# Block-decay attention into an ELU feed-forward layer: the state term on 64x64 array tiles, states without zero blocks, and one sum read from PSUM

## The chip, the core and the metric

One core of a Trainium2 chip. TensorE (PE) multiplies, with the weight loads listed apart (PEld); VectorE (DVE) and ScalarE (ACT) read PE's results out of PSUM; GpSimd (POOL) works on SBUF and issues most loads; SyncE (SP) issues stores and DMA transposes. The metric is device time of one run in microseconds, lower is better.

## The reference

q, k, v are [4, 8, 768, 64] (batch, head, position, channel), lam [8], w_in [512, 2048], w_out [2048, 512], all float32. Per batch and head, over blocks of 64 positions:

```python
intra = (q_b k_b^T * Dmask) v_b             # Dmask[i, j] = lam**(i-j) for i >= j, else 0
inter = (q_b * lam**(pos+1)) @ kv_state
out_b = intra + inter
kv_state = lam**block * kv_state + (k_b * lam**(block-1-pos))^T v_b
```

The result, as x [3072, 512] (batch and position by head and channel), goes through `g = elu(x @ w_in)` and `g @ w_out`.

## The kernel before

**Chunks.** The kernel works in blocks of 128 positions: 6 blocks for each of 4 batches give 24 chunks g, with block g // 4 and batch g % 4. Chunks 0 to 3 stand alone; from 4 on two neighbours form a pair with a common tile xt. Heads lie in pairs (hp 0 to 3, hh 0 or 1): head 2*hp + hh sits in partitions hh*64 onward of column block hp.

**Steps of a chunk or pair**, by the token that stands for each in the program list:
- loads of q, k, v (cast to fp16 by the DMA), issued on POOL;
- `T`: q and k transposed by PE and evicted by DVE (qT, times the decay qs) and ACT (kT), for chunks up to 7; from chunk 8 on two DMA transposes on SP, issued with `W`;
- `W`: those transposes, kd = k times decay on POOL (L176), and the scaled old state stt (L390, on POOL in four ops of 64 partitions, from chunk 12 on ACT, L383);
- `S`: 16 score matmuls per pair (L304), masked by DVE into pp (L320);
- `B` or `P`, the burst: for each hp two matmuls of v by pp (L340) and, from chunk 4 on, two of the state by qT (L346), into one PSUM bank psO per chunk; then U, the state's increment (L417), one bank per pair. The evictions are xt (L361 on ACT, from chunk 8 L363 on DVE, times qs) and the new state st (L440, two ops of 64 partitions);
- `1:g:j`: x @ w_in (L660) into a bank psH of two, then exp (L666) and relu (L667) on ACT, and min(e - 1, relu) on DVE (L626), giving g or gg;
- the product with w_out: `2:g:j`, plain, 16 matmuls of 512 columns per chunk (L685), evicted by ACT (L700); or, for the pairs in SEVEN (8 to 22 before), `7:g:i`.

A state tile st is [128, hp, 128]: for a head pair the two 64x64 states stand on the diagonal and the other two blocks are zeros, written at the start (`z`, L202 and `Z`, L704). So one state matmul contracts over 128 partitions, half of them against zeros.

**Seven products.** For a pair the product with w_out is a 2x2 block product (two chunks by two halves of w_out's columns, over two halves of the inner blocks) done by seven block products in the order M3, M4, M5, M2, M1, M7, M6, of 8 matmuls with 256 columns each (L549). The left sides are gg and its sums P (for M5, M2), E (for M1) and D (for M7, M6), by DVE or by POOL as SHARED says for each pair (L500, L497). The right sides wf are sums of w_out (`F` on DVE, `G` on POOL, L517). M5 is added in PSUM onto M3, M2 onto M4 and M6 onto M1. On the way: ACT copies M3, M4 and M1 to SBUF (L556) and M3+M5, M4+M2 into the output tile osb (L566); POOL makes t = M3 + M4 and two differences s1, s2 (L562); DVE makes w1 = s1 + M1 (L562), and the last two corners w1 - M7 and s2 + (M1+M6) from PSUM (L579).

**What sets the order.** Every engine works in the order of the program list: FIRST and OPEN, written by hand, then `1:` in order with one product token behind each, and the other steps set in at fixed distances (AT, in numbers of `1:` steps) before the pair that needs them. POOL's early order is POOL_ORDER (q, k, v loads, i and o for parts of w_in and w_out, d for kd, m for stt). DVE work that may wait stands in three lists (`late`, `slow`, `later`) of which `flush` takes some at each product token. psO, psS, psU, psT and psM share banks A to D, M0, M1 by BANKS. SP's queue follows the program: a store there waits for its data and holds what stands behind it.

Of the kernel before, what the change touches and what calls it, by code (L numbers as in the profile page):

```python
# [15 lines left out]
def kernel(  # L16
# [15 lines left out]
    L = 128  # L32
# [11 lines left out]
    WI = [2] * 8  # L44
    WO = [2] * 8
    POOL_ORDER = (
        "q1 k0 iota k2 k1 q2 v0 v1 i0 i1 v2 i3 i2 o0 o1 d0 k3 q3 i4 i5 d1 o2 d2 o3 d3 o4 v3 o5 "
        "i6 i7 k4 o7 o6 q4 k6 m4 v4 q6 d5 d4 q8 q10 k8 d6 v6 v8 d7 v10 k10 m6"
# [4 lines left out]
        "z3 z0 z1 Z2 Z1 z2 Z0 T0 T1 S0 S1 T2 P0 P1 S2 1:0:0 U0 1:1:0 P2 1:1:1 1:2:0 2:0:0 "  # L53
        "1:2:1 2:1:0 1:0:1 T3 2:2:0 1:0:2 S3 1:2:2 2:2:1 U1 1:1:2 2:1:1 2:0:1 P3 2:0:2 1:3:0 "
        "2:1:2 1:1:3 M 1:2:3 Z3 2:2:2 1:3:2 U2 1:3:1 2:1:3 1:0:3 T4 T5 2:2:3 1:3:3 S4:5 2:3:0 "
        "2:0:3 2:3:2 U3 F0 B:P4:P5:U4:U5 M 2:3:3 1:4:1 T6 1:4:0 G3 T7 2:3:1 G4 W9 1:4:3 G5 G1 "
        "S6:7 1:4:2 G2 2:5:0 2:4:0 1:4:4 1:4:5 W8 B:P6:P7:U6:U7 L12 1:4:7 1:6:1 2:5:1 2:4:1 G7 "
        "1:4:6 1:6:0 G6 2:4:2 S8:9 1:6:2 1:6:4 2:5:2 2:5:3 W11 1:6:3 1:6:6 B:P8:P9:U8:U9 1:6:7 "
        "2:4:3 1:6:5 W10"
# [4 lines left out]
    DELAY = 0  # L64
    COMB = nc.gpsimd

    SEVEN = (8, 10, 12, 14, 16, 18, 20, 22)
    SHARED = {8: 'D', 10: 'ED', 12: 'ED', 14: 'ED', 16: '', 18: '', 20: '', 22: 'ED'}
    AT = {'L': -19, 'l': 1, 'W': -13, 'T': -5, 'S': -7, 'B': -5}
    BANKS = (  # L70
        "S0=M0,A S1=D,C S2=D,M1 S3=D,B P0=M1 P1=M0 P2=B P3=A U0=B U1=B U2=B U3=M1 T0=M1,D "
        "T1=D,C T2=M0,D T3=B T4=B T5=D T6=M1 T7=D M2=C M3=M0"
# [19 lines left out]

    stp = [
        [cpool.tile([128, 2, NHP, 128], FP16, name=f"st{x}_{i}") for i in range(2)]
# [5 lines left out]
    def emit_load(w, g0):  # L100
        n = size_of[g0]
        c, b = divmod(g0, B)
        x = {"q": q, "k": k, "v": v}[w]
        src = x[b : b + n, :, c * L : (c + 1) * L].rearrange("b h p d -> p (b h) d")
        t = asb.tile([128, n, H, 64], FP16, tag=f"{w}n{n}", name=f"{w}n{g0}", bufs=4)
        {"q": qg, "k": kg, "v": vg}[w][g0] = t
        nc.gpsimd.dma_start(out=t[:].rearrange("p b h d -> p (b h) d"), in_=src)  # L107
# [38 lines left out]
    def emit_wi(i):  # L146
        written.add(("i", i))
        f0 = sum(WI[:i]) * 128
        nc.gpsimd.dma_start(  # L149
            out=wi16[i][:],  # L150
            in_=moe_w_in[:, f0 : f0 + WI[i] * 128].rearrange("(k p) f -> p k f", p=128),
        )
# [48 lines left out]
    def zero_st1(b):  # L201
        nc.vector.memset(st[b][1], 0.0)  # L202

# [8 lines left out]

    dn = cpool.tile([128, H], FP32, name="dn")
    mask = cpool.tile([128, H, 128], FP32, name="mask")
    qs = cpool.tile([128, NHP, 128], FP32, name="qs")
    ks = cpool.tile([128, H], FP32, name="ks")
# [11 lines left out]
    for hh in range(2):  # L228
        r = slice(hh * 64, (hh + 1) * 64)
        nc.vector.tensor_copy(loglam_p[r, :], loglam[r, hh::2])  # L230
    nc.vector.tensor_scalar_add(pos[:, 2:3], pos[:, 1:2], float(L))

    def emit_qs():
        for hp in range(NHP):
            nc.scalar.activation(
                qs[:, hp, :], row[:], AF.Exp, scale=loglam_p[:, hp : hp + 1]
            )
# [90 lines left out]

    def att_P(g):
        cb, b = divmod(g, B)  # L330
        until(E_done, g)
        if cb > 0:
            until(Y_done, g - B)
        vt = of(vg, g)
        qt, _ = qkT[g]
        po = bank(f"P{g}", 0, [128, NHP, 128], FP32, f"psO{g}")
        R = [slice(0, 64), slice(64, 128)]
        for hp in range(NHP):
            for hh, r in enumerate(R):
                nc.tensor.matmul(  # L340
                    po[r, hp, :], lhsT=vt[:, 2 * hp + hh, :], rhs=Pt[(g, hh)][:, hp, :],
                    start=True, stop=(cb == 0), skip_group_check=True,
                )
            if cb > 0:
                for r in R:
                    nc.tensor.matmul(  # L346
                        po[r, hp, :], lhsT=st[b][cb % 2][:, hp, r], rhs=qt[:, hp, :],
                        start=False, stop=True, skip_group_check=True,
                    )

        def evacuate():
            g0 = GFIRST[g]
            n = GSIZE[g0]
            if g0 not in xg:
                xg[g0] = asb.tile(
                    [128, NHP, n * 128], FP16, tag=f"xt{n}", name=f"xt{g0}",
                    bufs=4 if n == 1 else 2,
                )
            dst = xg[g0][:, :, (g - g0) * 128 : (g - g0 + 1) * 128]
            if g < GPE:  # L360
                nc.scalar.copy(out=dst, in_=po[:])  # L361
            else:
                nc.vector.tensor_tensor(out=dst, in0=po[:], in1=qs[:], op=ALU.mult)  # L363
            X_done.add(g)

        return [evacuate]

    stt = {}

    def att_M(g):  # L370

        cb, b = divmod(g, B)
        if cb == NCB - 1 or b % 2:
            return
        assert {f"U{g - B}", f"U{g - B + 1}"} <= seen
        until(Y_done, g - B)
        until(Y_done, g - B + 1)
        old = stp[b // 2][cb % 2]
        tmp = asb.tile([128, 2, NHP, 128], FP32, tag="stt", name=f"stt{g}", bufs=2)
        stt[g] = tmp  # L380
        if g >= MACT:
            for hp in range(NHP):
                nc.scalar.activation(  # L383
                    tmp[:, :, hp, :], old[:, :, hp, :], AF.Copy, scale=upp[:, hp : hp + 1]
                )
            return
        for hh in range(2):
            r = slice(hh * 64, (hh + 1) * 64)
            for x in range(2):
                nc.gpsimd.tensor_tensor(  # L390
                    out=tmp[r, x, :, r], in0=old[r, x, :, r],
                    in1=upp[r].unsqueeze(2).broadcast_to([64, NHP, 64]), op=ALU.mult,
                )
# [5 lines left out]
    def att_U(g, pu=None):  # L399
# [13 lines left out]
        else:  # L413
            for hp in range(NHP):
                for hh in range(2):
                    r = slice(hh * 64, (hh + 1) * 64)
                    nc.tensor.matmul(  # L417
                        pu[r, hp, :], lhsT=kds[g][:, 2 * hp + hh, :], rhs=vt[:, 2 * hp + hh, :],
                        start=True, stop=True, skip_group_check=True,
                    )  # L420
# [4 lines left out]
        def update(hh):  # L425
            r = slice(hh * 64, (hh + 1) * 64)
            nc.vector.tensor_copy(new[r, :, r], full[r, :, r])
            if hh == 1:
                Y_done.add(g)
# [3 lines left out]
    def updates(g, pu):  # L433
# [4 lines left out]
        def update(hh):  # L438
            r = slice(hh * 64, (hh + 1) * 64)
            nc.vector.tensor_tensor(  # L440
                out=new[r, :, :, r], in0=stt[g][r, :, :, r], in1=pu[r], op=ALU.add
            )
            if hh == 1:
                Y_done.update((g, g + 1))

        return [lambda: update(0), lambda: update(1)]

    def burst(*ops):

        us = [int(o[1:]) for o in ops if o[0] == "U" and int(o[1:]) // B < NCB - 1]  # L450
        evs, i = [], 0
        for o in ops:
            if o[0] == "P":
                evs += att_P(int(o[1:]))
# [67 lines left out]
    def mm2_seven(g0, i):  # L522
# [6 lines left out]
        z = seven[g0]  # L529
        if i < 2:  # L530
# [27 lines left out]
        def comb(n, in0, in1, op, into=None, eng=None):  # L558
            z[n] = z[into] if into else msb.tile(
                [128, 256], FP32, tag=n, bufs=1, name=f"{n}_{g0}"  # L560
            )
            (eng or COMB).tensor_tensor(out=z[n][:], in0=in0, in1=in1, op=op)  # L562
# [25 lines left out]
        elif m == 4:  # L588
            keep("m4")
            comb("t", z["m3"][:], z["m4"][:], ALU.add)  # L590
        elif m == 5:
            corner(0, R_)
            comb("s1", z["t"][:], z[0][:, R_], ALU.subtract, "m3")
        elif m == 2:
            corner(1, L_)
            comb("s2", z["t"][:], z[1][:, L_], ALU.subtract, "m4")
        elif m == 1:
            keep("m1")
            late.insert(
                0, lambda: comb("w1", z["s1"][:], z["m1"][:], ALU.add, "m1", nc.vector)  # L600
            )
# [101 lines left out]
    def zero_st(b):  # L703
        nc.scalar.memzero(st[b][0])  # L704

# [8 lines left out]
    def ready(t):  # L714
# [4 lines left out]
        if t[0] == "U" and g < 2 * B:  # L719
            assert f"{'z' if g < B else 'Z'}{g % B}" in seen  # L720
# [4 lines left out]
    def run(t):  # L725
# [11 lines left out]
        if w in "PUzZ":  # L737
            ready(t)
        if w == "S":
# [4 lines left out]
            late.pop(0)()  # L744
            late.pop(0)()
# [6 lines left out]
        else:  # L752
            {"T": att_T_pe, "1": mm1, "2": mm2, "Z": zero_st, "z": zero_st1,
             "q": lambda g, e: cast_raw(g, "q", e), "k": lambda g, e: cast_raw(g, "k", e),
             "7": mm2_seven, "F": w_sums, "G": lambda i: w_sums(i, nc.gpsimd), "c": lambda i: (emit_qs, emit_mask, emit_ks)[i](), "W": pool_work,
# [94 lines left out]
```

## Time and profile before

| | |
|---|---|
| median of 13 runs (lowest, highest) | 217.34 us (214.71, 220.07) |
| the profiled execution, run | 217.34 us |
| its span, first to last instruction | 215.6 us |
| PE busy, matmuls | 195.5 us, 2224 |
| DVE, ACT, POOL busy | 162.8, 140.5, 160.8 us |
| granted PE clock | 1.0 |

One line of a group reads: line, engine, operation, tile out<-in, shapes, count, busy us and mean ns of one, then the idle time of the engine just before them and what ended it. A matmul's own duration holds its way through the array; what a stream of them costs is the distance from one start to the next. A line of a timeline begins with start and duration in us. Waits are listed as engine and line, what was waited for, us in total, times, longest.

### The profile page before, as it was taken

What the parts mean: (1) busy time and instruction counts of PE and PEld (TensorE: products, weight loads), DVE (VectorE), ACT (ScalarE), POOL (GpSimd) and SP (SyncE); (2) the same over time, 40 slices, a digit from 0 to 9 for tenths busy, and PEclk for the clock granted to TensorE, in tenths of its full rate; (3) what the DMA queues carried; (4) which work ended last, traced back from release to release, by engine and by line L of the source; (5) the groups of instructions that cost most, each with busy time, mean ns of one, the idle gap of its engine ahead of it and who ended that gap; (6) DMA issues with size and microseconds to landing.
All of it is one profiled execution on the core that took longest, in us unless ns stands there. A gap on an engine that the chain in (4) does not pass through costs nothing.

```text
span 215.6 us, 5659 instructions
## 1 busy us (share of the span) xinstructions
PE 195.5 (91%) x2224; PEld 156.2 (72%) x2224; DVE 162.8 (76%) x294; ACT 140.5 (65%) x285; POOL 160.8 (75%) x187
## 2 busy tenths in 40 slices
PE   0786999999999994999999999989999999999983
PEld 0464767858576762767887887878887888888862
DVE  3864571689947783998988979898999979886622
ACT  4547565865785872767876976866667667667730
POOL 7998799999999999486899999995270401205961
PEclk9999999999999999999999999999999999999999
DMA  8999999999992499459909969969999911011022
GB/s 90 137 167 188 199 194 184 158 185 186 153 127 73 30 166 170 30 77 110 148 16 149 111 104 156 165 47 132 128 99 171 119 52 49 3 49 49 3 111 84
DMA packets 102122, 24.61 MB, mean 114 GB/s; under 512 B 92624, under 2 KB 99280, under 8 KB 102096
## 3 DMA queue, kind: packets, MB, share of 16 engines
q0 software_dynamic: 79760, 13.50, 83.0%
q1 hardware_dynamic: 22336, 10.76, 28.6%
q8 instruction: 17, 0.28, 0.6%
q14 instruction: 9, 0.07, 0.2%
HBM read 27.27 MB, written 6.29 MB: 156 GB/s over the span
## 4 chain that ended last, share of the span: by engine, by line
PE 69%; DMA 9%; DVE 8%; ACT 6%; POOL 5%; issue 2%; ACTq 0%; DVEq 0%; POOLq 0%; SPq 0%
PE psH L660 31%; PE psM L549 19%; PE psM L685 10%; DMA kT<-kn 4%; DMA wo<-in_moe_w_out_dram 4%; DVE gg L626 3%; PE psS L304 3%; ACT e L666 3%; ACT psH L667 3%; PE psO L340 2%; PE psO L346 2%; POOL wi L149 1%; POOL vn L107 1%; POOL kn L107 1%; DVE m L562 1%
## 5 line engine op out<-in xcount | busy, mean ns | idle before, releaser
L660 PE MATMUL psH<-xt,wi 128*128 128x256 f16 (+1 forms) x896 | 99.6, 258 | 4.1 <-DVE gg L626 2.3
L660 PEld LDWEIGHTS <-wi 128*128 128x128 f16 x896 | 77.7, 98 | 19.3 <-issue 5.1
L666 ACT ACTIVATE e<-psH 128x512 f32<-128x512 f32 x96 | 57.3, 597 | 49.6 <-PE psH L660 48.5
L667 ACT ACTIVATE psH<-psH 128x512 f32<-128x512 f32 x96 | 57.0, 593 | 0.0
L626 DVE SCALAR_TENSOR_TENSOR gg<-e,psH 128x512 f16<-128x512 f32 x64 | 43.5, 680 | 13.8 <-ACT psH L667 13.6
L320 DVE TENSOR_TENSOR pp<-psS,mask 128x512 f16<-128x512 f32 x48 | 31.3, 681 | 6.4 <-PE psS L304 6.4
L626 DVE SCALAR_TENSOR_TENSOR g<-e,psH 128x512 f16<-128x512 f32 x32 | 21.9, 684 | 18.4 <-ACT psH L667 18.2
L685 PE MATMUL psM<-wo,g 128*128 128x512 f16 x128 | 32.1, 379 | 0.8 <-DMA wo<-in_moe_w_out_dram 0.8
L497 POOL TENSOR_TENSOR fd<-gg 128x512 f16<-128x512 f16 x20 | 24.6, 1232 | 3.9 <-DVE gg L626 3.9
L176 POOL TENSOR_TENSOR kd<-kn,ks 128x512 f16<-128x512 f16 x20 | 21.5, 1076 | 1.8 <-DMA kn<-in_k_dram 1.7
L497 POOL TENSOR_TENSOR fe<-gg 128x256 f16<-128x256 f16 x16 | 12.2, 764 | 13.1 <-DVE gg L626 12.9
L517 POOL TENSOR_TENSOR wf<-wo 128x256 f16<-128x256 f16 (+1 forms) x28 | 21.1, 797 | 0.1
L562 POOL TENSOR_TENSOR t<-m,m 128x256 f32<-128x256 f32 x8 | 5.8, 726 | 19.6 <-ACT m L556 19.6
L685 PEld LDWEIGHTS <-g 128*128 128x128 f16 x128 | 11.7, 98 | 10.7 <-issue 1.2
L562 POOL TENSOR_TENSOR m<-t,osb 128x256 f32<-128x256 f32 x16 | 11.5, 726 | 9.9 <-ACT osb L566 6.0
L549 PE MATMUL psM<-wf,gg 128*128 128x256 f16 x128 | 16.8, 273 | 0.8 <-DVE osb L579 0.5
L549 PE MATMUL psM<-wo,fp 128*128 128x256 f16 x128 | 16.5, 273 | 0.0
L549 PE MATMUL psM<-wf,fd 128*128 128x256 f16 x128 | 16.4, 273 | 0.0
L500 DVE TENSOR_TENSOR fp<-gg 128x512 f16<-128x512 f16 x32 | 15.3, 479 | 0.6
L107 POOL DMA_DIRECT2D qn<-in_q_dram x13 | 14.7, 1135 | 0.9 <-POOLq L834 0.8
L107 POOL DMA_DIRECT2D kn<-in_k_dram x14 | 15.4, 1098 | 0.0
L107 POOL DMA_DIRECT2D vn<-in_v_dram x14 | 15.3, 1099 | 0.0
(60 smaller groups left out, 256.1 us busy)
## 6 DMA issues: line engine op xcount, KB each, us to landing
out_dram<-osb SPq DMA_DIRECT2D x22, 256.0 KB, 2.9
kn<-in_k_dram POOLq DMA_DIRECT2D x10, 256.0 KB, 7.7
qn<-in_q_dram POOLq DMA_DIRECT2D x10, 256.0 KB, 5.4
vn<-in_v_dram POOLq DMA_DIRECT2D x10, 256.0 KB, 8.9
wi<-in_moe_w_in_dram POOLq DMA_DIRECT2D x8, 256.0 KB, 7.4
wo<-in_moe_w_out_dram POOLq DMA_DIRECT2D x8, 256.0 KB, 9.0
kn<-in_k_dram POOLq DMA_DIRECT2D x4, 128.0 KB, 4.0
vn<-in_v_dram POOLq DMA_DIRECT2D x4, 128.0 KB, 5.8
```

The source lines that it names most:

```text
L107: nc.gpsimd.dma_start(out=t[:].rearrange("p b h d -> p (b h) d"), in_=src)
L176: nc.gpsimd.tensor_tensor(out=kd[:], in0=of(kg, g), in1=ks[:].unsqueeze(2).broadcast_to([128, H, 64]), op=ALU.mult,)
L320: nc.vector.tensor_tensor(out=P[:], in0=pts[hh][:], in1=mask[:, hh::2, :], op=ALU.mult)
L497: nc.gpsimd.tensor_tensor(out=out[:], in0=in0, in1=in1, op=op)
L517: eng.tensor_tensor(out=out, in0=in0, in1=in1, op=op)
L549: nc.tensor.matmul(out, lhsT=lhs, rhs=rhs, start=(s == 0 and m in (3, 4, 1, 7)), stop=(s == NFT // 2 - 1), skip_group_check=True,)
L562: (eng or COMB).tensor_tensor(out=z[n][:], in0=in0, in1=in1, op=op)
L626: nc.vector.scalar_tensor_tensor(out=g.rearrange("p f c t -> p (f c t)"), in0=e[:], scalar=-1.0, in1=r[:], op0=ALU.add, op1=ALU.min,)
L660: nc.tensor.matmul(pH[:, f * n * 128 : (f + 1) * n * 128], lhsT=wi16[i][:, kk, w * 128 : (w + 1) * 128], rhs=xg[g0][:, kk, :], start=(kk = ...
L666: nc.scalar.activation(e[:], pH[:], AF.Exp)
L667: nc.scalar.activation(pH[:], pH[:], AF.Relu)
L685: nc.tensor.matmul(psM[g][:, cols], lhsT=gts[(g, j * FB + f)], rhs=wo16[i][:, w, cols], start=first and f == 0, stop=end and f == FB - 1, ...
```

## The change

- **State term.** st becomes [128, hp, 64] without zero blocks, with head e + 2*hp in partition half e. A pair's state matmuls take 64 rows and 64 columns each, four with different row and column halves in a row, into two banks, one for the even and one for the odd heads of both chunks. All 16 state matmuls stand ahead of the 16 of v by pp, which add onto them. In xt the halves of a column block now hold heads hp and hp + 4; so w_in's rows are regrouped: a load takes 256 rows as 64 partitions by 4, for 512 columns, and the eviction multiplies by qx, a table in the new order (`c3`).
- **State update** is one DVE op instead of two, scaling one POOL op instead of four; the zeroing goes.
- **M1** is not copied: w1 = u + M1 reads PSUM, where u is the former s1 in a tile of its own. M6 can't begin until w1 is done.
- **Order and shares.** POOL_ORDER, OPEN, BANKS, AT change; w_sums(0) moves from DVE to POOL; W10 and W11 move ahead; pair 20 leaves SEVEN for the plain product; SHARED gives POOL the P sums of pairs 8, 12, 16 and 22.

```diff
-    WI = [2] * 8
+    WI = [4] * 4
     POOL_ORDER = (
-        "q1 k0 iota k2 k1 q2 v0 v1 i0 i1 v2 i3 i2 o0 o1 d0 k3 q3 i4 i5 d1 o2 d2 o3 d3 o4 v3 o5 "
-        "i6 i7 k4 o7 o6 q4 k6 m4 v4 q6 d5 d4 q8 q10 k8 d6 v6 v8 d7 v10 k10 m6"
+        "q1 k2 k0 iota q2 k1 i0 v0 v1 i1 v2 i3 i2 o0 k3 o1 q3 d0 i4 i5 d1 v3 o2 o3 i6 o4 d2 o5 "
+        "i7 k4 o7 o6 q4 v6 d3 k6 v4 q6 m4 k8 q10 d4 q8 d5 d7 d6 v8 m6 v10 k10"
     OPEN = (
-        "z3 z0 z1 Z2 Z1 z2 Z0 T0 T1 S0 S1 T2 P0 P1 S2 1:0:0 U0 1:1:0 P2 1:1:1 1:2:0 2:0:0 "
...
-        "1:4:6 1:6:0 G6 2:4:2 S8:9 1:6:2 1:6:4 2:5:2 2:5:3 W11 1:6:3 1:6:6 B:P8:P9:U8:U9 1:6:7 "
-        "2:4:3 1:6:5 W10"
+        "T0 S0 T1 T2 S1 P0 S2 P1 1:0:0 1:1:0 U0 P2 1:1:1 U1 1:2:0 2:0:0 1:2:1 2:1:0 1:0:1 T3 "
...
+        "L12 S8:9 W10 W11 1:6:2 1:6:4 2:5:2 2:5:3 1:6:6 G1 1:6:3 B:P8:P9:U8:U9 1:6:7 2:4:3 "
+        "1:6:5"
-    DELAY = 0
+    DELAY = 1
-    SEVEN = (8, 10, 12, 14, 16, 18, 20, 22)
-    SHARED = {8: 'D', 10: 'ED', 12: 'ED', 14: 'ED', 16: '', 18: '', 20: '', 22: 'ED'}
-    AT = {'L': -19, 'l': 1, 'W': -13, 'T': -5, 'S': -7, 'B': -5}
+    SEVEN = (8, 10, 12, 14, 16, 18, 22)
+    SHARED = {8: 'PD', 10: 'ED', 12: 'PE', 14: 'ED', 16: 'PD', 18: '', 22: 'PE'}
+    AT = {'L': -21, 'l': 1, 'W': -11, 'T': -7, 'S': -7, 'B': -5}
@@ emit_wi
+        i, hf = divmod(i, 2)
+        f0, r0 = sum(WI[:i]) * 128, hf * 256
         nc.gpsimd.dma_start(
-            out=wi16[i][:],
-            in_=moe_w_in[:, f0 : f0 + WI[i] * 128].rearrange("(k p) f -> p k f", p=128),
+            out=wi16[i][hf * 64 : hf * 64 + 64],
+            in_=moe_w_in[r0 : r0 + 256, f0 : f0 + WI[i] * 128].rearrange(
+                "(k p) f -> p k f", p=64
+            ),
@@ (new)
+    def scores_v(po, g, h, alone):
+        nc.tensor.matmul(
+            po, lhsT=of(vg, g)[:, h, :], rhs=Pt[(g, h % 2)][:, h // 2, :],
+            start=alone, stop=True, skip_group_check=True,
+        )
+    def att_P2(g):
...
+        po = [bank(f"P{g + e}", 0, [128, 2, 2, 128], FP32, f"psO{g}_{e}") for e in range(2)]
+        for a in range(2):
+            for i in range(2):
+                for c in range(2):
+                    for e in range(2):
+                        nc.tensor.matmul(
+                            po[e][R[c], a, i, :],
+                            lhsT=st[(g + i) % B][cb % 2][R[e], 2 * c + a, :],
+                            rhs=qkT[g + i][0][R[e], 2 * c + a, :],
+                            start=(a + i == 0), stop=False, skip_group_check=True,
+                        )
+        for i in range(2):
+            for h in (0, 4, 1, 5, 2, 6, 3, 7):
+                scores_v(po[h % 2][R[h // 4], h % 4 // 2, i, :], g + i, h, False)
+        def evacuate(e):
+            dst = xt_of(g)[:, e::2, :]
...
+                    out=dst.rearrange("p a (i t) -> p a i t", i=2), in0=po[e][:],
+                    in1=qx[:, e::2, :].unsqueeze(2).broadcast_to([128, 2, 2, 128]),
@@ att_M
-        for hh in range(2):
-            r = slice(hh * 64, (hh + 1) * 64)
-            for x in range(2):
-                nc.gpsimd.tensor_tensor(
-                    out=tmp[r, x, :, r], in0=old[r, x, :, r],
-                    in1=upp[r].unsqueeze(2).broadcast_to([64, NHP, 64]), op=ALU.mult,
-                )
+        nc.gpsimd.tensor_tensor(
+            out=tmp[:], in0=old[:], op=ALU.mult,
+            in1=upp[:].unsqueeze(1).unsqueeze(3).broadcast_to([128, 2, NHP, 64]),
+        )
@@ updates
-        def update(hh):
-            nc.vector.tensor_tensor(
-                out=new[r, :, :, r], in0=stt[g][r, :, :, r], in1=pu[r], op=ALU.add
-            )
+        def update():
+            nc.vector.tensor_tensor(out=new[:], in0=stt[g][:], in1=pu[:], op=ALU.add)
@@ mm2_seven
+        while i == 6 and "w1" not in z:
+            late.pop(0)()
...
         elif m == 1:
-            keep("m1")
-            late.insert(
-                0, lambda: comb("w1", z["s1"][:], z["m1"][:], ALU.add, "m1", nc.vector)
-            )
+            late.insert(0, lambda: comb("w1", "u", None, ALU.add, nc.vector))
```

## The prediction

> **What bounds the kernel now.** First the page's busy shares, then the waits of TensorE (PE), then the order of time around the waits that are long.
>
> ```profile
> PE 195.5 (91%) x2224; PEld 156.2 (72%) x2224; DVE 162.8 (76%) x294; ACT 140.5 (65%) x285; POOL 160.8 (75%) x187
> ...
> L660 PE MATMUL psH<-xt,wi 128*128 128x256 f16 (+1 forms) x896 | 99.6, 258 | 4.1 <-DVE gg L626 2.3
> ```
>
> PE is busy for 91% of the span, at full granted clock, so the time is PE's matmuls plus its waits. Adding up matmuls by their start-to-start distance (109 ns for 256 columns, 55.6 for 128, 215.6 for 512) gives 184.1 us of bare work; the first starts at 5.6 and the last ends at 212.2. So about 22 us inside PE's stretch are waits, cold start and mode changes. The waits, in total us, times, longest:
>
> ```profile
> PE psT L285 <- DVE qn L125: 5.6, 1, 5.6
> PE psS L304 <- DMA kT<-kn: 2.9, 1, 2.9
> PE psH L660 <- DVE gg L626: 2.3, 7, 1.1
> PE psM L685 <- DMA wo<-in_moe_w_out_dram: 0.8, 2, 0.5
> PE psM L549 <- DVE osb L579: 0.5, 1, 0.5
> ```
>
> One long wait after the start: scores of chunks 10 and 11 wait for kT. SP's timeline (start, us) shows why:
>
> ```profile
> 65.92 7.70 SPq L610 DMA_DIRECT2D out_dram<-osb  x2
> 73.72 1.27 SPq L270 DMA_TRANSPOSE qT<-qn  x1
> 75.05 1.31 SPq L270 DMA_TRANSPOSE kT<-kn  x1
> ```
>
> Two stores that wait for their data hold SP 7.70 us; the transposes of chunk 10 stand behind them, meet the loads of chunk 12 that POOL issued at 71.8 to 74.1, and land after 9.4 us, at 84.5. The second find is on DVE in the steady stage, where a sum of two fp32 tiles in SBUF (w1) took 2.50 us instead of its usual 0.42, while POOL worked, and PE stood 1.07 us:
>
> ```profile
> 142.44 2.50 DVE L562 TENSOR_TENSOR m<-m,m 128x256 f32<-128x256 f32 x1
> 145.59 1.96 PE L660 MATMUL psH<-xt,wi 128*128 128x256 f16 x16 [1.07 <-DVE gg L626]
> ```
>
> **The change part by part.** All against the profiled execution: span 215.6, run 217.34 (1.74 us lie around the span). That run equals the median of the 13 shown.
>
> *State term.* The burst of attention matmuls:
>
> ```profile
> 48.86 0.22 PE L340 MATMUL psO<-pp,vn 128*64 128x128 f16 x2
> 48.92 0.22 PE L346 MATMUL psO<-qT,st 128*64 128x128 f16 x2
> 48.98 0.22 PE L340 MATMUL psO<-pp,vn 128*64 128x128 f16 x2
> ...
> 49.42 0.42 PE L417 MATMUL psU<-vn,kd 128*64 128x64 f16 x16
> ```
>
> Two column tiles start every 55.5 ns, so 16 state matmuls per pair of chunks take 0.445 us, in 10 bursts (160 in all). As 64x64 tiles, still 16 of them, four at once would be 4 x 55.5 = 0.22. No row shows such a tile. Nearest are the 16 L417 matmuls, half as long, which take 0.35 us: 22 ns each although two at a time need less. I take that floor: 16 x 22 = 0.35. The row-tiled scores (L304, 16 in 0.55 us, 34 ns each) are the dear end: 0.55. The burst gets one more change of array mode, from 64x64 to 128x64 rows. Rows bound it at 0.025 (first pair of a burst 0.08 instead of 0.055) and 0.11 (the first L549 group after scores takes 0.98 in the chain, others 0.87); I take 0.05, as the new change lies inside a burst like the first. Net per burst 0.35 + 0.05 - 0.445 = -0.045, in 10 bursts -0.4; ends -2.0 and +2.2.
> The Trainium skill ("TensorEngine Tiling (Array Packing)", Key Properties and Instruction Overhead) speaks against this part: a change of tiling mode drains TensorE, and each matmul carries about 60 cycles, so that small ones stop shrinking. At 2.4 GHz that is an estimated 25 ns a matmul, 0.40 us a burst, and with the same switch a net of zero instead of -0.4; the trace agrees that there is a floor, at 22 ns.
>
> *kT of chunks 10 and 11.* W10 and W11 move ahead of the two stores on SP. Their k load lands at 64.6 (SP's kT issue waited for it until 64.63) and still comes last of its batch; qT has five buffers: chunk 11 takes that of chunk 6, free after burst 6 at 61.6. So they issue at 65 to 68 and land by 77 even at the 9.4 us of before; PE wants them at about 81. PE's wait of 2.9 goes. Late next would be POOL, which was continuously busy to 85.8: it loses about 5 us (four state scalings, 16 x 0.64 = 9.9 us on half the partitions, become 4 of about 1.2, the nearest 128x512 rows being 1.08 and 1.23) and gains w_sums(0), 3.0 us, so it reaches the first sum at about 83, when that is due at 84. -2.9; ends -3.0 and -1.0. The stores now stand behind the transposes; nobody waits for them.
>
> *Start.* POOL issues k2 ahead of k0 and iota, so iota is 0.9 us later, and two small copies join DVE: the first transpose at 6.8 instead of 5.6. It is hidden: 1:1:1 waits for w_in until 18.41, and the same twelve loads stand before it. What isn't hidden: k3 moves ahead of o1, and v3 ahead of o2 and o3. kd3 started on k3's landing at 22.68, 0.9 after o1's 21.80: a load costs the queue 0.9. 2:0's second half starts at 22.65 (+0.85, of which 0.2 is filled by U1 moved ahead); o3 lands one load later, near 28.2, and is wanted 1.8 us of PE work earlier: +0.6 more. Sum +1.2; ends 0 (order absorbs it) and +2.5 (loads of w_in by 64 partitions land slower; before 5.6 to 9.5 us after issue). The removed zeroing (4 x 0.27 on DVE, 4 x 0.4 on ACT) is slack; qx, four times 0.39 on ACT, lies where ACT is busy 2.6 of 5 us.
>
> *w_sums(0)* leaves DVE (2.4 us at 49.5 to 51.9), where PE lost 0.85 us between bursts 4 and 6: -0.4 (0 to -0.85).
>
> *M1 from PSUM.* ACT loses eight copies of 0.375 (slack). w1 on DVE then has one operand in PSUM, like L579: 0.41, never 0.8 or 2.5, so the 1.07 stall goes: -1.0. Added wait: M6 adds onto M1's place in its bank, so PE's M6, and all of PE behind it, waits for w1, and w1 for POOL's u. Before, w1 ran at 142.44 with M6 at 143.49, but at 159.59 with M6 at 159.90: 0.1 to 0.2 missing in the stages with all sums on DVE. +0.3 (0 to +1.5). The state update, one DVE op for two of 0.68, gives DVE 0.68 per pair: slack.
>
> *Group 20 as a plain product:* 32 x 215.6 = 6.90 instead of 56 x 109 = 6.10 us of PE: +0.8. At the end PE waited 0.32 for gg and 0.50 for an osb that freed group 20's bank; the second goes, as plain products free theirs by a copy two slots earlier: -0.4 (ends 0, -0.8).
>
> DELAY 1 for 0 does nothing: it is counted down before it is tested, both fire at the first flush.
>
> Sum: -0.4 - 2.9 + 1.2 - 0.4 - 1.0 + 0.3 + 0.8 - 0.4 = -2.8. Span 212.8, run **214.5** (-1.3%).
>
> **The rivals.**
> *Row tiles don't run side by side* (slower; this is also "the change doesn't do what it says"). If 64x64 matmuls overlap only within one row half, or each pays its own switch, 16 cost 16 x 55.5 = 0.89: +0.49 per burst with the switch, 10 bursts +4.9 in place of -0.4. Run 214.5 + 5.3 = 219.8. It decides from 0.23 us per burst above my 0.40: then the whole gain is gone. For it: scores run at 34 ns, above the 28 that two at once would give. Against: they do run below 55.5. Chance 0.15.
> *POOL becomes the bound* (no change). From 103 to 148 POOL ran without a gap: eight sums 7.8, three loads 3.5, two kd 2.1, t, s1, s2 2.2, together 15.6 per 15.5 us stage. The change adds P forms in stages 8 and 16, some 5 us each, into POOL gaps of 6.6 (86 to 103) and of as much after 148, and makes P, due two products earlier than D, its work in stages 12, 16 and 22. Should P cost 0.15 more than D, a stage is 0.6 longer, over five stages 3.0: run 217.5. For it: fd ran 1.14 to 1.34 beside DVE. Against: fp8_3 at about 99 is due at 103. Chance 0.12.
> *Loads late at the start* at the dear end of that term (+1.3) and the DVE gains at zero (+0.4, and w1's stall kept, +1.0): 217.2, no change. Chance 0.08.
>
> **How the numbers follow.** Forecast 0.65: 211.9 (state tiles at 0.22 and the end's stall fully gone) to 216.2 (M6 and start at two thirds of their dear ends). The range reaches to the POOL and load rivals and a part of the first: 211.9 to 218.5. 0.5% (1.1 us) is about what a measurement can tell from no change: faster below 216.25. Faster 0.67 (forecast, and a sliver of the others), same 0.13 (most of the two no-change rivals), slower 0.2 (first rival, and what of POOL's goes past its price).
>
> **What would show it.** Right: no kT wait of PE; a burst of 32 + 16 matmuls within 1.3 us (1.38 before); w1 near 0.41 each time; 2:0's second half at 22.5 to 23; last PE end near 209.5. Wrong: state matmuls over 40 ns apart; PE waiting for POOL at fp or fe; PE waiting for DVE w1 at M6 by over 0.3 us a group; DMA waits of w_in or w_out above 3 us.

## The result and the profile after

The changed kernel takes 219.71 us (median of 11 runs, 218.62 to 224.35) against 217.30 us (48 runs of the kernel before): ratio 1.0152, 95% interval 1.0121 to 1.0184. It is slower by 1.5%; the forecast was 214.5, 1.3% faster. The profiled execution took 219.49 us with a span of 217.7. The kernels ran in several sessions, so they are compared by their ratio to the kernel before in the same session, and by the spans of the profiled executions. The ratios leave out runs more than 1.5% above the fastest of their kernel, but in the session of e1, e2, e3 and e8 this keeps eight runs of the kernel before with a lowered clock (0.992), so that the ratios of e1, e2 and e8 come out some 0.6% low.

Busy shares of the page, then TensorE's (PE's) waits (total us, times, longest):

```profile
PE 195.8 (90%) x2200; PEld 152.6 (70%) x2200; DVE 153.5 (71%) x253; ACT 136.1 (63%) x275; POOL 168.2 (77%) x188
```

```profile
PE psH L718 <- DVE gg L684: 6.8, 11, 1.5
PE psT L301 <- DVE qn L130: 6.8, 1, 6.8
PE psO L358 <- DMA vn<-in_v_dram: 1.1, 2, 0.5
PE psH L718 <- DMA wi<-in_moe_w_in_dram: 0.7, 1, 0.7
```

PE has as much work as before (195.5). The kT wait (2.9) is no longer in the list; the wait for gg, which was 2.3, is 6.8. DVE (VectorE) is *less* busy than before (153.5 instead of 162.8), so more work on it is not the reason: something holds it up. PE's timeline (start, us) shows what went as planned, the burst of pair 4 and the scores of pair 10:

```profile
49.47 0.42 PE L388 MATMUL psO<-qT,st 64*64 64x128 f16 x16
49.82 0.64 PE L358 MATMUL psO<-pp,vn 128*64 128x128 f16 x16
50.29 0.42 PE L459 MATMUL psU<-vn,kd 128*64 128x64 f16 x16
...
81.32 0.62 PE L320 MATMUL psS<-qT,kT 64*128 64x128 f16 x16
```

The state term takes 0.35 us (49.47 to 49.82), the burst with U 1.17 instead of 1.27, and the scores start at 81.32 instead of 84.52. So the kernel is 3.2 us *ahead* there, and 5.3 us worse after that. On DVE, with PE's wait behind it:

```profile
155.54 3.04 DVE L544 TENSOR_TENSOR fe<-gg 128x256 f16<-128x256 f16 x1
158.51 0.67 DVE L482 TENSOR_TENSOR st<-stt,psU 128x512 f16<-128x512 f32 x1
159.11 1.27 DVE L684 SCALAR_TENSOR_TENSOR gg<-e,psH 128x512 f16<-128x512 f32 x2
```

```profile
159.84 1.03 PE L718 MATMUL psH<-xt,wi 128*128 128x256 f16 x8 [1.47 <-DVE gg L684]
```

A sum fe, 0.28 us where nothing disturbs it, took 3.04; the eviction gg behind it on DVE was late, and with it PE's bank psH. GpSimd (POOL) in the same stretch:

```profile
152.44 1.21 POOL L541 TENSOR_TENSOR fd<-gg 128x512 f16<-128x512 f16 x1
153.60 0.72 POOL L638 TENSOR_TENSOR t<-m,m 128x256 f32<-128x256 f32 x1
154.27 1.20 POOL L109 DMA_DIRECT2D qn<-in_q_dram  x1
155.48 1.16 POOL L541 TENSOR_TENSOR fp<-gg 128x512 f16<-128x512 f16 x1
156.59 1.15 POOL L541 TENSOR_TENSOR fd<-gg 128x512 f16<-128x512 f16 x1
157.71 0.72 POOL L649 TENSOR_TENSOR u<-t,osb 128x256 f32<-128x256 f32 x1
158.38 1.17 POOL L109 DMA_DIRECT2D kn<-in_k_dram  x1
```

POOL works without a gap, and fe ends (158.58) only when POOL's tensor operations do (158.43). It waited not for one of them but for three.

The table is worked out from PE's timelines: the start of the score matmuls of pair 10, then the time in us from the scores of one pair to those of the next. A stage without loss takes 15.2 to 15.5. The kernels e1 to e20 follow in the next section.

| kernel | pair 10 at | 10–12 | 12–14 | 14–16 | 16–18 | 18–20 | 20–22 | span |
|---|---|---|---|---|---|---|---|---|
| before | 84.52 | 15.44 | 15.61 | 15.50 | 16.41 | 15.51 | 15.25 | 215.6 |
| changed | 81.32 | 16.91 | 15.40 | 15.68 | 17.57 | 18.66 | 15.15 | 217.7 |
| changed, old table (e1) | 81.00 | 16.93 | 16.54 | 17.95 | 17.95 | 16.59 | 15.15 | 219.1 |
| changed, group 16 off POOL (e2) | 81.96 | 16.90 | 15.40 | 15.68 | 17.57 | 16.89 | 15.15 | 216.6 |
| changed, no sums on POOL (e13) | 81.02 | 15.73 | 16.45 | 16.55 | 16.56 | 15.53 | 15.15 | 214.0 |
| changed, old places (e12) | 81.03 | 17.82 | 15.40 | 15.41 | 15.40 | 15.40 | 15.15 | 212.6 |
| changed, only kd back (e19) | 81.70 | 19.16 | 15.40 | 18.14 | 16.21 | 17.15 | 16.65 | 221.4 |
| changed, only loads back (e20) | 81.22 | 15.35 | 16.95 | 15.40 | 16.01 | 15.39 | 15.15 | 212.5 |
| changed, no sums, old places (e17) | 81.47 | 15.34 | 15.72 | 15.71 | 15.71 | 15.46 | 15.15 | 211.6 |

### The profile page after: what moved, and what is told of

Same layout as the page of the kernel before. It is cut to its first block, busy times and chain, and to the rows that moved or that the text cites. A ratio compares the mean times of both kernels' runs of the same rounds, so it can differ in the third digit from the quotient of the medians.

```text
span 217.7 us, 5560 instructions
## 1 busy us (share of the span) xinstructions
PE 195.8 (90%) x2200; PEld 152.6 (70%) x2200; DVE 153.5 (71%) x253; ACT 136.1 (63%) x275; POOL 168.2 (77%) x188
## 4 chain that ended last, share of the span: by engine, by line
PE 73%; DVE 8%; issue 5%; ACT 5%; DMA 4%; POOL 3%; DVEq 0%; ACTq 0%; POOLq 0%
PE psH L718 35%; PE psM L595 16%; PE psM L743 14%; DVE gg L684 4%; DMA wi<-in_moe_w_in_dram 4%; PE psO L358 3%; ACT psH L725 2%; PE psS L320 2%; ACT e L724 2%; PE psO L388 1%; POOL kn L109 1%; DVE pp L336 1%; DVE st L482 1%; PE psU L459 1%; POOL qn L109 1%
## 5 line engine op out<-in xcount | busy, mean ns | idle before, releaser
L684 DVE SCALAR_TENSOR_TENSOR gg<-e,psH 128x512 f16<-128x512 f32 x56 | 37.8, 680 | 19.4 <-ACT psH L725 19.4
L684 DVE SCALAR_TENSOR_TENSOR g<-e,psH 128x512 f16<-128x512 f32 x40 | 27.4, 684 | 25.7 <-ACT psH L725 24.0
L743 PE MATMUL psM<-wo,g 128*128 128x512 f16 x160 | 40.0, 379 | 0.0
L541 POOL TENSOR_TENSOR fp<-gg 128x512 f16<-128x512 f16 x16 | 19.9, 1244 | 17.4 <-DVE gg L684 17.2
L561 POOL TENSOR_TENSOR wf<-wo 128x256 f16<-128x256 f16 (+1 forms) x32 | 24.1, 784 | 0.0
L743 PEld LDWEIGHTS <-g 128*128 128x128 f16 x160 | 14.9, 98 | 11.9
L541 POOL TENSOR_TENSOR fd<-gg 128x512 f16<-128x512 f16 x16 | 19.0, 1189 | 0.0
L595 PE MATMUL psM<-wf,gg 128*128 128x256 f16 x112 | 14.6, 273 | 0.3 <-DVE gg L684 0.3
L595 PE MATMUL psM<-wo,fp 128*128 128x256 f16 x112 | 14.4, 273 | 0.0
L595 PEld LDWEIGHTS <-gg 128*128 128x128 f16 x112 | 10.4, 98 | 2.6 <-DVE gg L684 0.6
```

The costliest lines, as they stand in the source:

```text
L541: nc.gpsimd.tensor_tensor(out=out[:], in0=in0, in1=in1, op=op)
L561: eng.tensor_tensor(out=out, in0=in0, in1=in1, op=op)
L595: nc.tensor.matmul(out, lhsT=lhs, rhs=rhs, start=(s == 0 and m in (3, 4, 1, 7)), stop=(s == NFT // 2 - 1), skip_group_check=True,)
L684: nc.vector.scalar_tensor_tensor(out=g.rearrange("p f c t -> p (f c t)"), in0=e[:], scalar=-1.0, in1=r[:], op0=ALU.add, op1=ALU.min,)
L743: nc.tensor.matmul(psM[g][:, cols], lhsT=gts[(g, j * FB + f)], rhs=wo16[i][:, w, cols], start=first and f == 0, stop=end and f == FB - 1, ...
```

## The experiments

Theory A: a DVE sum of two tiles in SBUF is held up while POOL works through a run of tensor operations. Rivals: B, the rest of the new order (M6 behind w1, combinations); D, DVE too slow for the sums; and, for smaller parts, the start, pair 20 and the array tiles.

### Which sums POOL has

**e1_old_split**

```diff
-    SHARED = {8: 'PD', 10: 'ED', 12: 'PE', 14: 'ED', 16: 'PD', 18: '', 22: 'PE'}
+    SHARED = {8: 'D', 10: 'ED', 12: 'ED', 14: 'ED', 16: '', 18: '', 22: 'ED'}
```

> The changed kernel with the old table of which sums POOL computes (SHARED: D in 8, ED in 10, 12, 14 and 22, none in 16 and 18). Theory A (DVE's sum of two tiles in SBUF is held up while POOL works through a run of tensor operations; gg stands behind it on DVE and TensorE's psH behind gg): no sum of stages 8 and 16 above 1.3 us, TensorE's waits for gg fall from 6.8 us to 1 to 2.5, time 214.5 to 216. Theory B (the rest of the new order costs it: product M6 waiting for w1, the combinations on POOL, the places of the sums): waits for gg stay above 5 us, time 219 to 220.5.

221.37 us, ratio 1.017 (1.0114 to 1.0227): no gain, and PE's wait for gg is 8.4. Theory A in this simple form (more sums on POOL, more loss) missed. In the stages 10 to 16 two fp in each are stretched (2.66 and 2.56, 2.70 and 2.56, 2.70 and 2.56 us), with the very table under which the kernel before had none of them. So it isn't the table alone.

**e2_no_pool_16** (the changed kernel)

```diff
-    SHARED = {8: 'PD', 10: 'ED', 12: 'PE', 14: 'ED', 16: 'PD', 18: '', 22: 'PE'}
+    SHARED = {8: 'PD', 10: 'ED', 12: 'PE', 14: 'ED', 16: '', 18: '', 22: 'PE'}
```

> The changed kernel with one entry altered: group 16's sums all on DVE, as in the kernel before; groups 8, 12 and 22 stay as changed. A: the two stalls after 149 us (0.96 and 1.47) go, stage 16 is some 3 us shorter, time 216.5 to 217.5, and the stall at 92.5 (1.41) stays. B: 219 to 220.5, with a wait of PE on DVE of over 2 us still in stage 16.

218.41 us, ratio 1.0042 (0.9999 to 1.0085), between the two ranges; by the profiled spans (216.6 against 217.7) 0.5% below the changed kernel. The stage 18–20, where group 16's products lie, falls from 18.66 to 16.89; 16–18 stays at 17.57, where I had expected both to shorten, and of the two stalls after 149 us that of 0.96 is still there (0.95).

**e3_before_pool_16** (the kernel before)

```diff
-    SHARED = {8: 'D', 10: 'ED', 12: 'ED', 14: 'ED', 16: '', 18: '', 20: '', 22: 'ED'}
+    SHARED = {8: 'D', 10: 'ED', 12: 'ED', 14: 'ED', 16: 'PD', 18: '', 20: '', 22: 'ED'}
```

> The kernel before with one entry altered: POOL computes P and D of group 16, as the change has it. A: DVE's fe of group 16 is stretched to 2 us or more at least twice and PE waits for gg behind it, time up by 1.5 to 3.5 us, 218.8 to 220.8. B (the loss needs the new order, M1 in PSUM and the new places): 217.3, within 0.6.

220.43 us, ratio 1.0131 (1.0079 to 1.0184). By the table's measure the edit costs 1.23 us (18–20: 16.74 instead of 15.51): w1 took 2.66 us, fe 0.93 and 0.92, where I had expected fe at 2 us or more. The other 2.9 us of this execution lie in 10–12 (18.30 instead of 15.44), ahead of the edit, where the granted clock was low (below, under hardware). So in the kernel before, too, a DVE sum of two tiles in SBUF is held beside POOL's sums, but it is w1 and not fe, and the edit accounts for 1.23 of the 3.8 us between the two profiled spans (219.4 and 215.6).

**e13_no_pool_sums** (the changed kernel)

```diff
-    SHARED = {8: 'PD', 10: 'ED', 12: 'PE', 14: 'ED', 16: 'PD', 18: '', 22: 'PE'}
+    SHARED = {8: '', 10: '', 12: '', 14: '', 16: '', 18: '', 22: ''}
```

> The changed kernel with no sums on POOL in any group (SHARED empty): DVE computes P, E and D of all seven groups, POOL keeps t, u, s2, kd and the loads. Theory A, sharpened after the first runs (a two-operand sum of DVE is held when its start falls together with the start of a run of POOL operations; which sums POOL has matters less than that it has any at that moment): no sum above 1.3 us but for single ones beside kd, waits for gg below 2.5 us, time 213.5 to 216. Rival D (DVE is too slow for all the sums; that is why POOL was given some): each of the stages 8 to 14 takes 1 us or more longer than now, time 219 to 223, with waits for gg above 7 us.

216.55 us, ratio 1.0012 (0.9972 to 1.0052): 1.4% below the changed kernel. The waits for gg fall from 6.8 to 0.9 and no sum takes over 1.13 us. D's price (219 to 223) is not reached: DVE with all the sums gives stages of 16.5, a us longer than the best of the changed kernel, and the loss there has another name, w1 late for M6:

```profile
110.49 1.03 PE L595 MATMUL psM<-wf,fd 128*128 128x256 f16 x8 [1.19 <-DVE u L609]
127.04 1.03 PE L595 MATMUL psM<-wf,fd 128*128 128x256 f16 x8 [1.24 <-DVE u L609]
143.59 1.03 PE L595 MATMUL psM<-wf,fd 128*128 128x256 f16 x8 [1.24 <-DVE u L609]
```

**e14_before_w10_no_pool** (every entry of SHARED empty, as in e13, in the kernel of e8 below)

> The kernel before with the transposes of chunks 10 and 11 ahead of the stores (214.4 by itself) and no sums on POOL. If POOL's sums cost there too (w1 stretched to 2.5, sums of 1.24): 212.5 to 214, w1 never above 1. If POOL's help pays where its runs begin 0.25 us or more ahead of DVE's sums: 215 to 217.5, with DVE busy and waits for gg above 4 us in stages 10 to 14.

214.95 us, ratio 0.9982 (0.9959 to 1.0004), with a profiled span of 213.2, where e8 had 214.43, 0.985 (0.9798 to 0.9902) and 212.8. Three stages, from pair 12 to 18, take 15.90 each (in e8 15.61, 15.50 and 16.42). Under the old places POOL's sums cost the kernel before nothing.

### Where loads and kd stand

**e11_old_split_old_places**

```diff
-    AT = {'L': -21, 'l': 1, 'W': -11, 'T': -7, 'S': -7, 'B': -5}
+    AT = {'L': -19, 'l': 1, 'W': -13, 'T': -5, 'S': -7, 'B': -5}
```

with e1's table. (`T` acts on nothing here: from chunk 8 on the transposes go with `W`.)

> The changed kernel with both the old table of POOL's sums and the old places of loads and kd in the order (L -19, W -13, T -5). In the kernel before, with these, DVE's fp began 0.25 to 0.38 us after POOL's fe and got in at the next boundary; with the old table alone it began 0.05 to 0.09 after and waited for the whole run. If the places of kd and loads set that phase: fp back to 0.57 to 0.70, time 215 to 216.5. If the phase comes from what is not undone (combinations u and s2, one state update, order of the opening): still 2.5 us and more twice in a stage, time 219.5 to 221.5.

217.0 us, ratio 1.0005 (0.9956 to 1.0053): 1.65% below e1, by the places alone. fp is back at 0.42 to 0.69 in most stages; two fp still took 2.88 and 3.48 us, and PE waited 3.6 us for pp behind them, so the time came out above the 216.5 that I had set.

**e12_old_places** (the diff of e11, with the changed kernel's own table of sums)

> The changed kernel with only the places of loads and kd as before (L -19, W -13, T -5) and the new table of POOL's sums. If the places alone set when POOL's runs meet DVE's sums: 216.5 to 218, waits for gg below 4 us, though group 16 keeps its loss. If table and places work only together: 219 to 222, as with the old table alone (221.4).

214.49 us, ratio 0.9938 (0.9892 to 0.9985): 2.1% below the changed kernel, and faster than the kernel before. Four stages run at 15.40. M1 in PSUM, the combinations and the opening are as changed here, so of rival B only the places are left. PE's waits:

```profile
PE psT L301 <- DVE qn L130: 6.8, 1, 6.8
PE psO L358 <- DVE pp L336: 2.3, 1, 2.3
PE psS L320 <- ACT kT L309: 1.4, 2, 0.7
PE psH L718 <- DVE gg L684: 1.3, 6, 0.2
```

Group 16 keeps its P and D on POOL here and does not lose, against what I had expected. POOL and DVE at the place of the 3.04-us sum above:

```profile
151.91 1.16 POOL L541 TENSOR_TENSOR fp<-gg 128x512 f16<-128x512 f16 x1 [1.18 <-DVE gg L684]
153.02 1.21 POOL L541 TENSOR_TENSOR fd<-gg 128x512 f16<-128x512 f16 x1
154.18 0.73 POOL L649 TENSOR_TENSOR u<-t,osb 128x256 f32<-128x256 f32 x1
154.99 0.73 POOL L609 TENSOR_TENSOR t<-t,osb 128x256 f32<-128x256 f32 x1
155.66 1.18 POOL L109 DMA_DIRECT2D qn<-in_q_dram  x1
```

```profile
151.98 1.23 DVE L544 TENSOR_TENSOR fe<-gg 128x256 f16<-128x256 f16 x1
```

It is the same meeting: fe starts 0.07 us after POOL's fp (0.06 in the changed kernel), so the delay between the two starts, which e11 went by, is not the difference. But the issue of the q load now stands behind the sums, so POOL had idled 1.18 us, waiting for gg, before its run began; and fe got in between fp and fd (1.23 instead of 3.04). In the changed kernel the load's issue, 1.20 us, filled that gap and tied t, qn, fp, fd and u into one run. The 2.3-us wait for pp that is left comes from one fe of 3.75 us at 83.86, behind a run of POOL from the sums of w_out (L561) to kd.

**e19_kd_back** and **e20_loads_back** (the changed kernel, one place put back in each)

```diff
-    AT = {'L': -21, 'l': 1, 'W': -11, 'T': -7, 'S': -7, 'B': -5}
+    AT = {'L': -21, 'l': 1, 'W': -13, 'T': -7, 'S': -7, 'B': -5}   # e19
+    AT = {'L': -19, 'l': 1, 'W': -11, 'T': -7, 'S': -7, 'B': -5}   # e20
```

> The changed kernel with only the place of the transposes and kd put back (W -13), loads two slots earlier as changed (L -21). In the changed kernel kd stood directly ahead of fe and fd in one run of POOL (145.40 to 148.17 us) and a DMA issue directly ahead of fp and fd (154.27 to 157.7). If kd's place decides: stages of 15.4 us, 214 to 215.5. If the loads' place decides: 218 to 221, with stretched sums behind a load's issue.

> The changed kernel with only the place of the loads put back (L -19), kd two slots later as changed (W -11). If the loads' place decides: stages of 15.4 us, 214 to 215.5. If kd's place decides: 218 to 221. If both are needed: each of the two runs lies between, 216 to 219.

With only kd put back (e19) 222.94 us, ratio 1.029 (1.0218 to 1.0361), with six sums of 2.1 to 3.4 us. With only the loads put back (e20) 216.01 us, ratio 0.9985 (0.9945 to 1.0025), waits for gg 1.3, and a profiled span of 212.5 (e12 212.6). The place of the loads decides: with it, most of the loss goes for either place of kd (1.7% here, 2.1% in e12); without it, moving kd back makes it worse. In e20 the meeting of e12 comes about once more:

```profile
150.99 0.72 POOL L638 TENSOR_TENSOR t<-m,m 128x256 f32<-128x256 f32 x1
151.76 1.15 POOL L541 TENSOR_TENSOR fp<-gg 128x512 f16<-128x512 f16 x1
```

```profile
151.85 1.21 DVE L544 TENSOR_TENSOR fe<-gg 128x256 f16<-128x256 f16 x1
```

Again fe is over in 1.21 us, and here POOL had stood still for only 0.05 us between t and fp (151.71 to 151.76). So it doesn't take a pause of a us. What e12 and e20 have in common against the changed kernel is that the load's issue does not stand directly ahead of fp.

**e17_no_pool_old_places** (the diffs of e11's places and of e13's table together)

> The changed kernel with no sums on POOL and with the old places of loads and kd. With the new places and no sums it ran 216.5 and PE waited 3.7 us for w1 at M6. If the places matter only through POOL's sums: 216 to 217. If kd next to fp and fe (1.04 and 1.12 in each stage) makes w1 late: kd moves away from them, M6's wait falls below 1.5 us, 214 to 215.5.

213.56 us, ratio 0.9893 (0.9858 to 0.9928): the fastest form of the changed kernel. The wait for w1 at M6 is gone: kd stretched fp to 1.04 and fe to 1.12 in three stages of e13, just ahead of w1; here it meets fe and fd elsewhere (0.6 and 0.66). So the places also matter without any sums on POOL. Rival D is out with this run: DVE has all the sums in the fastest form.

**e10_one_slot_later** (in `sums`, for groups with two sums on POOL)

```diff
+        if len(SHARED.get(g0, "")) == 2:
+            todo.insert(0, lambda: None)
         return todo
```

> The changed kernel; in groups 8 to 16 and 22 DVE's one remaining sum is issued one place later in DVE's order (behind the next evacuation), with the same sums on the same engines. If what counts is whether the sum meets the start of POOL's run: the stretched sums (3.07, 2.19, 2.69, 2.56, 3.04 us) change places or go; with POOL's two sums (2.3 us) over by then, most are 0.28 to 1.3, waits for gg 1 to 4 us, time 215.5 to 218.5. If only the amount of work on POOL counts: as many stretched sums as before, 219 to 221.

222.03 us, ratio 1.0228 (1.0163 to 1.0293), waits for gg 8.9. A miss: the stretched sums did change places, but there were more of them. To move DVE's sum blindly is no remedy when POOL's run is long.

### The rest of the sum

**e8_only_w10** (the kernel before)

```diff
-        "1:4:6 1:6:0 G6 2:4:2 S8:9 1:6:2 1:6:4 2:5:2 2:5:3 W11 1:6:3 1:6:6 B:P8:P9:U8:U9 1:6:7 "
-        "2:4:3 1:6:5 W10"
+        "1:4:6 1:6:0 G6 2:4:2 S8:9 W10 W11 1:6:2 1:6:4 2:5:2 2:5:3 1:6:3 1:6:6 B:P8:P9:U8:U9 1:6:7 "
+        "2:4:3 1:6:5"
```

> The kernel before with only the transposes (and kd) of chunks 10 and 11 moved ahead of the two stores on SP. If the kT wait was the stores' doing, PE's wait for kT (2.9 us) is gone and the time is 214.0 to 215.0. If the loads of chunk 12 hold the transposes anyway, kT lands late all the same and the time is 216.5 to 217.5; if POOL is late instead, PE waits for a sum or for kd by up to 2 us, 215 to 217.

214.43 us, ratio 0.985 (0.9798 to 0.9902). The scores of pair 10 start at 81.77, without a wait for kT's DMA. The profiled span is 212.8 us: one move of two tokens gives what the whole change was forecast to give.

**e4_state_two_at_once** (`att_P2` of the changed kernel)

```diff
         for a in range(2):
-            for i in range(2):
-                for c in range(2):
-                    for e in range(2):
+            for e in range(2):
+                for i in range(2):
+                    for c in range(2):
```

> The changed kernel with the state matmuls in another order: the two row halves one after the other (for a, for e, for i, for c), so that neighbours share their rows and differ only in columns and pass. If four tiles run at once and the order allows it only as written: the 16 take 0.445 us (27.8 ns each) in place of 0.35. If 22 ns is what the issue of one costs: 0.35 all the same, time within 0.5 of the changed kernel.

The 16 state matmuls take 0.35 us (49.72 to 50.07) in this order as well; ratio 1.0179 (1.0107 to 1.0252), the changed kernel's within the intervals. 22 ns is what one costs whatever its neighbour's rows.

**e7_m1_copied** (the changed kernel) and **e16_no_pool_sums_m1_copied** (the same with e13's table)

```diff
         elif m == 1:
-            late.insert(0, lambda: comb("w1", "u", None, ALU.add, nc.vector))
+            keep("m1")
+            def w1():
+                z["w1"] = z["u"]
+                nc.vector.tensor_tensor(
+                    out=z["w1"][:], in0=z["u"][:], in1=z["m1"][:], op=ALU.add
+                )
+            late.insert(0, w1)
```

> The changed kernel with M1 copied out by ACT again, so that w1 adds two fp32 tiles in SBUF. The prediction's step (w1 with one operand in PSUM is never stretched, worth 1.0 us): w1 above 1 us at least twice in stages 8 to 16, time 0.5 to 2 us above the changed kernel, 220.2 to 221.7. If w1 was only one of many and no dearer than others: within 0.5 of the changed kernel.

> The changed kernel with no sums on POOL and with M1 copied out by ACT again, so that product M6 does not wait for w1's read of PSUM. In the run without POOL's sums PE waited 3.7 us for w1 at M6 (three times, up to 1.2). If that wait is the price of reading M1 from PSUM: it is gone, w1 stays below 1 us as POOL is quiet, and the time is 1.5 to 3.5 us below that run, 213 to 215. If DVE is late in any case and PE only waits elsewhere: 216 to 217.5, with waits for gg or for pp in its place.

e7: 222.97 us, ratio 1.0247 (1.0187 to 1.0306), 0.9% above the changed kernel; w1 took 1.59, 1.05, 3.01 and 3.36 us in four groups. e16: 216.02 us, ratio 0.9999 (0.9959 to 1.004), as e13: the wait at M6 goes, 3.5 us of waits for gg come. Reading M1 from PSUM is worth about 2 us beside a busy POOL and nothing beside a quiet one.

**e5_old_opening_loads** (the changed kernel; the rest of POOL_ORDER as it is)

```diff
-        "q1 k2 k0 iota q2 k1 i0 v0 v1 i1 v2 i3 i2 o0 k3 o1 q3 d0 i4 i5 d1 v3 o2 o3 i6 o4 d2 o5 "
+        "q1 k0 iota k2 k1 q2 v0 v1 i0 i1 v2 i3 i2 o0 o1 d0 k3 q3 i4 i5 d1 o2 o3 v3 i6 o4 d2 o5 "
```

> The changed kernel with the old order of POOL's early work (iota and k0 ahead of k2, o0 and o1 ahead of k3, o2 and o3 ahead of v3). If the order of the loads makes the start late: first transpose at 5.6, first product 1:0:0 near 14, second half of 2:0 near 22, time 1 to 2 us below the changed kernel, 217.7 to 218.7. If the w_in loads by half the partitions are what is slow: 1:0:0 at 16 to 17 all the same, and the time within 0.5 of the changed kernel.

221.01 us, ratio 1.0177 (1.0114 to 1.0241), no gain; the first transpose is early (5.89), but 1:0:0 starts at 15.62 after a 1.2-us wait for w_in.

**e15_half_partition_loads** (the kernel before)

```diff
-    WI = [2] * 8
+    WI = [4] * 4
@@ emit_wi
+        i, hf = divmod(i, 2)
-            out=wi16[i][:],
-            in_=moe_w_in[:, f0 : f0 + WI[i] * 128].rearrange("(k p) f -> p k f", p=128),
+            out=wi16[i][hf * 64 : hf * 64 + 64],
+            in_=moe_w_in[:, f0 : f0 + WI[i] * 128].rearrange(
+                "(k h p) f -> h p k f", h=2, p=64
+            )[hf],
```

> The kernel before with w_in loaded as the change loads it: 512 columns for 64 partitions in one transfer, in place of 256 columns for 128 (same bytes, same number and order of loads, rows in their old places). If that form lands later: 1:0:0 moves from 13.85 to 15 to 16, POOL waits for a w_in load between issues, time 0.5 to 2 us above the kernel before. If the order alone made the start late: 1:0:0 within 0.3 of 13.85, time within 0.5.

1:0:0 starts at 15.15 instead of 13.85 with the order untouched, so the form of the load delays it by 1.3 us; yet the whole takes 217.65, ratio 0.9968 (0.9917 to 1.0018). By the scores of pair 8 only 0.4 us of the delay is left (68.83 against 68.44).

**e6_group20_seven** (the changed kernel)

```diff
-    SEVEN = (8, 10, 12, 14, 16, 18, 22)
-    SHARED = {8: 'PD', 10: 'ED', 12: 'PE', 14: 'ED', 16: 'PD', 18: '', 22: 'PE'}
+    SEVEN = (8, 10, 12, 14, 16, 18, 20, 22)
+    SHARED = {8: 'PD', 10: 'ED', 12: 'PE', 14: 'ED', 16: 'PD', 18: '', 20: '', 22: 'PE'}
```

> The changed kernel with group 20 again in seven products, all its sums on DVE. By the prediction's terms the plain product costs 0.8 us of PE and saves 0.4 at the end: 219.0 to 219.6, 0.1 to 0.7 below the changed kernel. If DVE's relief in group 20 is worth more than PE's 0.8 us: 220 to 221.

220.13 us, ratio 1.0189 (1.014 to 1.0237). The time says nothing on the 0.4 us asked about, since the stages before pair 20, where the two programs are the same, differ by more: 12–14 took 17.90 here and 15.40 in the changed kernel. In the last stretch alone, from the scores of pair 22 to the end, it took 37.2 us with seven products and 37.0 with the plain one, so the plain product costs nothing that can be seen. Where the meetings fall changes from one execution to the next.

## Why the prediction was wrong

**The step that failed.** The line of AT (loads two slots earlier, kd two later) has no term in the sum at all: the prediction costs the opening's order load by load and passes over the one line that moves the loads of every later stage. Put back alone (e12), it gives a ratio of 0.9938 instead of 1.0152 and a profiled span of 212.6 us, against 217.7 with the change and 212.8 forecast: about the whole error. That e12 comes so near the forecast is in part luck, as its stage 10–12 still loses 2.4 us that the forecast didn't have and other terms came out cheaper. The loss also needs the sums on POOL: without them, at the new places, the span is 214.0 (e13). Its price needed the second failing step: the 2.50-us w1, which the prediction shows, was read as w1's own trouble and priced at 1.0 us, gone with M1 in PSUM. It was one case of what can befall a sum of two tiles in SBUF, fp, fd and fe among them, beside a POOL that does not pause. POOL was looked at only as an engine that may be late (rival 2, 217.5); PE never waited for it.

That rival had the right engine and the wrong mechanism. "POOL ran without a gap" was the thing to follow, but to the engine beside it, DVE, and not to PE, which takes its results.

**Step by step.** *State term*: 22 ns and 0.35 us as assumed; the burst gained 0.10 instead of 0.045, so some -1.0 in ten bursts instead of -0.4. The first rival (0.89 per burst) is out. *kT*, for -2.9: between the scores of pairs 8 and 10 lie 16.1 us before, 13.1 in e8 and 12.8 in the changed kernel, which also gains at the burst there. *Start*: P3 begins at 31.72 instead of 32.26 with 1.75 us less of PE's work ahead of it, so +1.2 as said, but for another reason: the load form (+1.3 at 1:0:0 in e15, which the prediction held to be hidden) and not k3 and v3, whose old order gains nothing in e5. By the scores of pair 8 only 0.1 is left of it (68.56 against 68.44): 1.1 us were made up, of which w_sums(0) was to give 0.4. *w1*: 0.41 each time, as said, worth about 2 (e7) instead of 1.0. *M6*: no wait in the changed kernel; 3.7 where DVE carries all the sums (e13). *Pair 20 and the end*: from the scores of pair 22 to the end 37.0 us instead of 37.3; +0.4 was forecast.

**What the traces say of the hold.** Over all twenty traces, from 84 us on, count the DVE sums of two SBUF tiles (fp, fe, fd, w1) that took over 0.1 us more than alone, by how long POOL had been working without a gap (of 0.1 us or more, DMA issues counted as work) when the sum began. Below 3.4 us: 149 sums, and none was held for over 1.0 us, that is, it got in when the running operation ended. From 3.4 us on: 160 sums, 70 held for over 1.0 us, 59 for 1.7 or more. A short pause seems to do: of 180 sums that met a POOL tensor operation begun after a pause of 0.03 us or more, none was held for over 1.0 us. This is counted afterwards, not tried, and many of the sums are the same place in nearly the same program: that the pause itself is the cause, and what lets 90 sums in early in a long run, stays open.

The Trainium skill ("SBUF — State Buffer", "SBUF: two separate sides") calls the pair of ports that DVE and GpSimd share an exclusive lock, taken by whichever starts first and held for the whole instruction, against a DVE instruction with two SBUF inputs among others. The traces agree that such sums wait and sums with an operand in PSUM don't (w1 0.41), but differ in length: fe stood through three POOL instructions, 2.76 us.

## What to carry to other kernels

When the operations of one engine can hold those of another, the amount of work on each doesn't tell the price. With the same sums on POOL and on DVE, the loads of a pair two places earlier in POOL's queue made the kernel 1.7% slower (e20 against the changed kernel; spans 212.5 and 217.7 us). So moving a DMA issue on POOL's queue is not free, even where no one waits for the load: look at what then stands directly behind it. And in a sum of terms, go through every changed line, the numbers in a table of places too, and when one operation is stretched, ask which others have the same form.

## What the runs showed of the hardware

- A sum of two fp16 tiles in SBUF on DVE, 0.28 to 0.42 us alone, took up to 3.75 us beside POOL's tensor operations.
- A 64x64 matmul of 128 columns costs 22 ns in a stream, in either order of rows and columns; behind them the 16 matmuls of v by pp took 0.47 us, against 0.44 at two every 55.5 ns, so the extra change of array mode costs 0.03 at most.
- Loading w_in by 64 partitions instead of 128, with the same bytes and order, put the first product 1.3 us later.
- A wait of PE for 2 to 3 us can be followed by half the clock. In e3's profile, stretches of 2 us (PE busy, weight loads, DVE, ACT, POOL, then the granted PE clock) around the kT wait:

```profile
82.00:84.00 2.00, 0.00 (x0) 0.00 (x0) 0.00 (x0) 0.75 (x2) 2.00 (x4) 0.85 1.70 137
84.00:86.00 2.00, 1.75 (x18) 1.06 (x19) 1.11 (x2) 0.00 (x0) 1.56 (x3) 0.50 0.98 240
86.00:88.00 2.00, 2.00 (x9) 1.10 (x8) 2.00 (x4) 0.00 (x0) 1.08 (x1) 0.50 1.34 64
88.00:90.00 2.00, 2.00 (x8) 0.99 (x7) 1.39 (x3) 1.09 (x2) 1.25 (x2) 0.50 0.08 12
```

The clock stayed at 0.50 until 90 us, in a stretch that is the same program as the kernel before, whose profiled execution kept 1.00 after a wait of 2.87. So a wait of this length may cost twice its length. The low stretches last 3.4 us in the traces of e11, e15 and e19 and 6.8 in e3's, each beginning inside the longest wait of PE or within 1 us of its end. A mean clock of 0.992 or less came in 47 of 107 runs of the kernel before beside the experiments (mean 218.6 us, the other 60 215.9) and in 27 of 48 runs of the five other kernels whose profile has a PE wait of 1.95 us or more after the start (e3, e11, e12, e15, e19), and in none of the 124 runs of the 14 kernels whose longest was 1.56 or less. So to take such a wait out is worth more than its length. The Trainium skill ("TensorE: Matmul & The Clock Gate", "What's actually happening") puts the halved clock down to an idle window of about 3.4 us that runs freely; the waits here are shorter, and the clock fell after some of them and not after others.
